# Chunked attention with a maxout layer in fp32: the last two token groups as one unit, their inner layers by seven block products for eight

## The chip, the cores and the metric

The kernel runs on one core of a Trainium2 chip. The metric is device microseconds of one execution. The engines are called as the profile calls them: PE is TensorE's matmul, PEld its weight load, DVE VectorE, ACT ScalarE, POOL GpSimd, SP SyncE, which issues the DMAs here.

## The reference

```python
# q, k, v: (8, 8, 576, 64) fp32; chunks of 64 positions
scores = scale * np.matmul(q_c, k_c.transpose(0, 1, 2, 4, 3))
attn = softmax(scores)                    # rows of 64, with 1e-9 added to the sum
x = (attn @ v_c) laid out as (4608, 512)  # tokens x d_model
h = np.maximum(np.maximum(x @ w1, x @ w2), x @ w3)   # 512 -> 768, three weights
out = h @ w_out                                      # 768 -> 512
```

Attention looks only inside a chunk, so 128 tokens of x (two chunks of all eight heads) can be made on their own. Then come three matrix products with an elementwise maximum, and one more product.

## The kernel before

**Precision.** A matmul operand is kept as two fp32r halves: a rounded high part and the rest, its low part. A product is then three matmuls, low times high, high times low and high times high, added up in one PSUM bank (`three`, L150 to L153). A high part is made on ACT by a cast, a low part by a subtraction on DVE or POOL.

**Tiles.** The 4,608 tokens are nine groups of 512. `wh` and `wl` hold the halves of the three weights in six column blocks of 128 (index j), `woh` and `wol` those of the last. For each group and each j, the three weights (index w) take 4 x 3 matmuls of 128x512 each into one bank (`hidden`). `maximum` evacuates the bank: ACT copies the first to the tile `m` (L431), DVE takes the greater of bank and `m` for the other two (L433). Then `high` (L439, ACT) and `low` (L442, DVE) make the halves `hh` and `hl`. After the six j, `project` multiplies these by `wout` in four blocks of 128 tokens, 6 x 3 matmuls each, and `output` copies and stores (L454, L455). A group has 288 such matmuls: 216 in the inner layers and 72 in the last.

**Attention.** A unit is 128 tokens, so 36 units. The first eight go through `plain_steps` in the first, hand-ordered stretch. The other 28 go through `attention`: loads of q and k (`r`), their halves (`qs`, `kk`), scores in two halves (`s`, L269) that share one PSUM buffer, evacuated by two ACT copies (L275) and two DVE additions (L280), the softmax steps, halves of the result (`ah`), a turn through DRAM (`there`, then `aa`), halves of v (`vs`, L287 and on POOL L291), two value products (`x`, L269) that share one buffer as well, and the halves of x (`xh`, `xl`, L394 and L399).

**Order.** The first stretch is the table `FIRST`. After it a list `parts` gives PE's matmuls, and every other step has a due time on a clock `now` that counts PE's work (0.6815 per three matmuls, 0.49 per attention product). A heap gives out the steps as they come due, and each engine runs its own in that order. Units of a group are due while the group ahead of it is on PE, 18.3 units of that clock apart. PSUM is used so: four banks in turn for the products, two for `s`, two for `x`.

## Time and profile before

| | us |
|---|---|
| median of 3 runs | 695.45 (695.07 to 703.29) |
| profiled execution, span from first to last instruction | 693.2 |
| the profiled execution's own time | not given; the nearest run, 695.07, is 1.9 above its span |
| PE busy | 687.0 (99%) |
| DVE, ACT, POOL busy | 449.2, 357.6, 150.7 |
| granted TensorE clock | 1.00 in the mean |

The share of an engine is its busy time by the span. The chain of waits names, for each stretch of the span, the engine on which the end depended. Rows of groups give a line, an engine, an operation and its tiles (written <- read), the number of instructions, the busy time, the mean ns of one, and the idle time ahead of them with what ended it. Rows of the timeline begin with the start and the duration in us. The first group lasts to about 120 us; from there to the end the eight other groups follow each other.

### The profile page before, as it was taken

How to read it: one execution, taken by the hardware profiler on the slowest of the kernel's cores; microseconds unless marked ns; L12 is line 12 of the kernel's file. 1: busy time of each engine (PE TensorE's matmuls, PEld its weight loads, DVE VectorE, ACT ScalarE, POOL GpSimd, SP SyncE). 2: the span in 40 equal slices, each digit the busy share in tenths (PEclk: the TensorE clock that was granted, in tenths of full speed). 3: DMA queues.
4: the chain of work that ended last, by engine and by line, in shares of the span. 5: the costliest groups of instructions: out<-in, count | busy, mean ns of one | idle time of the engine just before them, and what ended most of it. 6: DMA issues, size and time to landing. Idle time of an engine off the chain costs nothing.

```text
span 693.2 us, 9474 instructions
## 1 busy us (share of the span) xinstructions
PE 687.0 (99%) x3390; PEld 576.2 (83%) x3390; DVE 449.2 (65%) x805; ACT 357.6 (52%) x663; POOL 150.7 (22%) x107
## 2 busy tenths in 40 slices
PE   8999999999999999999999999999999999999997
PEld 5998888888888888888888888888888888888886
DVE  6999975767577766776577657775777567721220
ACT  4867645555655555555555555556555555431111
POOL 1422111212222222222222222221222222210000
PEclk9999999999999999999999999999999999999999
DMA  8955536455755576557655675557555765340001
GB/s 334 402 205 212 213 122 206 143 172 175 237 163 168 166 241 183 161 174 226 200 182 182 181 229 154 162 161 235 163 172 161 239 180 175 98 136 16 1 0 61
DMA packets 42351, 121.21 MB, mean 175 GB/s; under 512 B 3904, under 2 KB 3904, under 8 KB 42304
## 3 DMA queue, kind: packets, MB, share of 16 engines
q1 hardware_dynamic: 42304, 120.60, 54.3%
q8 instruction: 27, 0.44, 0.3%
q14 instruction: 20, 0.16, 0.1%
HBM read 96.47 MB, written 24.12 MB: 174 GB/s over the span
## 4 chain that ended last, share of the span: by engine, by line
PE 97%; DMA 2%; SPq 0%; ACT 0%; issue 0%
PE pm L151 29%; PE pm L153 28%; PE pm L152 28%; PE x L269 4%; PE s L269 4%; PE x L234 2%; PE s L191 1%; DMA buf<-in_vb 1%; DMA buf<-in_qk 1%; PE tp L223 0%; SPq L114 0%; ACT ao L454 0%; SPq L181 0%
## 5 line engine op out<-in xcount | busy, mean ns | idle before, releaser
L151 PE MATMUL pm<-xh,wl 128*128 128x512 f32 (+1 forms) x660 | 256.9, 389 | 0.0
L153 PE MATMUL pm<-xh,wh 128*128 128x512 f32 (+1 forms) x660 | 255.1, 386 | 0.0
L152 PE MATMUL pm<-xl,wh 128*128 128x512 f32 (+1 forms) x660 | 254.7, 386 | 0.0
L153 PEld LDWEIGHTS pm<-xh,wh 128*128 128x128 f32 x660 | 124.0, 188 | 26.5
L152 PEld LDWEIGHTS pm<-xl,wh 128*128 128x128 f32 x660 | 124.2, 188 | 22.1
L151 PEld LDWEIGHTS pm<-xh,wl 128*128 128x128 f32 x660 | 124.2, 188 | 22.0
L291 POOL TENSOR_TENSOR vs<-rv,vs 64x1024 fp32r<-64x1024 f32 x28 | 67.2, 2400 | 280.0 <-ACT vs L287 280.0
L280 DVE TENSOR_TENSOR e<-s,e 64x256 f32<-64x256 f32 x112 | 47.3, 422 | 102.5 <-ACT e L275 101.8
L433 DVE TENSOR_TENSOR m<-pm,m 128x512 f32<-128x512 f32 (+1 forms) x110 | 75.0, 682 | 38.1 <-PE pm L153 35.1
L151 PE MATMUL pm<-woh,hl 128*128 128x512 f32 x216 | 84.6, 392 | 0.0
L153 PE MATMUL pm<-woh,hh 128*128 128x512 f32 x216 | 84.3, 390 | 0.0
L152 PE MATMUL pm<-wol,hh 128*128 128x512 f32 x216 | 84.2, 390 | 0.0
L275 ACT COPY e<-s 64x256 f32<-64x256 f32 x112 | 41.2, 368 | 60.6 <-PE s L269 59.9
L275 ACT COPY xs<-x 64x256 f32<-64x256 f32 x112 | 41.1, 367 | 54.9 <-PE x L269 54.3
L439 ACT CAST hh<-m 128x512 fp32r<-128x512 f32 (+1 forms) x55 | 33.7, 613 | 69.2 <-DVE m L433 68.7
L280 DVE TENSOR_TENSOR xs<-x,xs 64x256 f32<-64x256 f32 x112 | 47.3, 422 | 25.2 <-ACT xs L275 23.5
L431 ACT COPY m<-pm 128x512 f32<-128x512 f32 (+1 forms) x55 | 31.8, 579 | 50.2 <-DVE hl L442 27.1
L153 PEld LDWEIGHTS pm<-woh,hh 128*128 128x128 f32 x216 | 40.5, 188 | 9.0
L152 PEld LDWEIGHTS pm<-wol,hh 128*128 128x128 f32 x216 | 40.6, 188 | 7.6
L151 PEld LDWEIGHTS pm<-woh,hl 128*128 128x128 f32 x216 | 40.6, 188 | 7.6
L168 POOL TENSOR_TENSOR e<-e,sm 128x512 f32<-128x512 f32 x30 | 31.3, 1043 | 68.3 <-DVE sm L165 68.3
L442 DVE TENSOR_TENSOR hl<-m,hh 128x512 fp32r<-128x512 f32 (+1 forms) x55 | 38.5, 699 | 5.7 <-ACT hh L439 4.8
(65 smaller groups left out, 756.6 us busy)
## 6 DMA issues: line engine op xcount, KB each, us to landing
r<-in_qk SPq DMA_DIRECT2D x56, 512.0 KB, 7.5
aa<-there SPq DMA_DIRECT2D x56, 512.0 KB, 5.9
rv<-in_v SPq DMA_DIRECT2D x28, 512.0 KB, 4.1
there<-ah SPq DMA_DIRECT2D x28, 512.0 KB, 2.6
out_x<-ao SPq DMA_DIRECT2D x36, 256.0 KB, 2.0
buf<-in_qk SPq DMA_DIRECT2D x8, 768.0 KB, 8.1
buf<-in_w SPq DMA_DIRECT2D x10, 512.0 KB, 4.1
buf<-in_vb SPq DMA_DIRECT2D x8, 512.0 KB, 5.7
```

What stands on the lines that cost most here:

```text
L151: nc.tensor.matmul(out=o, lhsT=al, rhs=bh, start=first, stop=False)
L152: nc.tensor.matmul(out=o, lhsT=ah, rhs=bl, start=False, stop=False)
L153: nc.tensor.matmul(out=o, lhsT=ah, rhs=bh, start=False, stop=last)
L168: eng.tensor_tensor(out=e, in0=e, in1=sm.unsqueeze(2).broadcast_to([P, 8, 64]), op=ALU.mult)
L269: nc.tensor.matmul(out=o[:, g].rearrange("p a h x -> p (a h x)"), lhsT=lhs(g), rhs=rhs(g), start=True, stop=True)
L275: nc.scalar.copy(out=out()[rows], in_=st[name][rows, :, 0, h, :])
L280: nc.vector.tensor_tensor(out=out()[rows], in0=st[name][rows, :, 1, h, :], in1=out()[rows], op=ALU.add)
L291: eng.tensor_tensor(out=st[name][64:], in0=src()[64:], in1=st[name][64:].bitcast(F32), op=ALU.subtract)
L431: nc.scalar.copy(out=banks[j][:, :n], in_=ps[j, w][:, :n])
L433: nc.vector.tensor_tensor(out=banks[j][:, :n], in0=ps[j, w][:, :n], in1=banks[j][:, :n], op=ALU.max)
L439: nc.scalar.copy(out=hh[j][:, lo:hi], in_=banks[j][:, :hi - lo])
L442: eng.tensor_tensor(out=hl[j][:, lo:hi], in0=banks[j][:, :hi - lo], in1=hh[j][:, lo:hi].bitcast(F32), op=ALU.subtract)
```

## The change

The last two groups, 1,024 tokens, become one unit (`pair`). Its inner layers are taken as 2x2 block matrices: two blocks of 256 input rows, two of 128 columns (blocks j = 2jp and 2jp+1), two of 512 tokens. Seven block products stand for the eight, in the variant with 15 block additions. One pair of column blocks jp and one weight w are a set; nine sets (jp 0 to 2, w 0 to 2), each 7 x 2 x 3 = 42 matmuls, where 48 stood.

- The tokens' side: b11, b21, b12, b22 are the four blocks of x in the tile `stage`. Four differences of them (`mix`, two on DVE, two on POOL) and the halves of seven operands (`high` on ACT, `low` on DVE, one on POOL) are made once (`operands`), each 128x1024.
- The weights' side (`combine`): per set, the two column blocks are made whole again from their halves (DVE; POOL for set 0), four sums of 128x256 on POOL, and their halves by ACT and DVE (the tile `c`).
- The results' side (`pair`'s `hidden`): per set, ACT copies products 1, 4, 5 and 7; DVE adds `u2` = product 6 + product 1; POOL makes `v`, `y` and `c22`; DVE makes c11, c12 and c21. For w > 0 DVE takes the greater with `m` four times, and for w = 2 the halves of the result follow (`H`, four casts and four subtractions).
- All 28 attention units are due ahead of the pair: the first four 18.0 apart as before, twelve 16.1 apart, twelve 14.0 apart. The last eight write their x into `stage`, unsplit.
- The pair's products go round eight banks (the four of `s` and `x` join). The last product of the pair starts with blocks 0 to 3 of three token blocks.
- Buffers move under other names; the scratch for DMA descriptors goes from 8192 to 1024. `FIRST` is the same.

```diff
+LATE = [0.0, 0.0, -1.2]
+EVERY = [18.3, 16.4, 14.6]
+OPERANDS = 5.0
+SECOND_MIXED = 1.6
+ORDER = (1, 2, 4, 5, 6, 3, 7)
+TIMES = [17.3 + 18.0 * n for n in range(4)] + [71.3 + 16.1 * (n + 1) for n in range(12)] + [282.0 + 14.0 * n for n in range(12)]
...
+    def combine(jp, w, homes, into, eng):
+
+        st = {}
+        a, b = 2 * jp, 2 * jp + 1
+        minus, plus = ALU.subtract, ALU.add
...
+        def whole(j, n):
+            def fn():
+                st[n] = homes[n]()
+                eng.tensor_tensor(out=st[n], in0=wh[j][:, w].bitcast(F32), in1=wl[j][:, w].bitcast(F32), op=plus)
+            return fn
...
+        def sum_of(n, x, y, op):
+            return lambda: nc.gpsimd.tensor_tensor(out=f32(n)(), in0=x(), in1=y(), op=op)
...
+        def high():
+            for k in range(2):
+                nc.scalar.copy(out=into()[:, 0, 2 * k:2 * k + 2], in_=st["c", k])
+
+        def low():
+            for k in range(2):
+                nc.vector.tensor_tensor(out=into()[:, 1, 2 * k:2 * k + 2], in0=st["c", k],
+                                        in1=into()[:, 0, 2 * k:2 * k + 2].bitcast(F32), op=minus)
+
+        return [whole(b, 1), whole(a, 0), sum_of(2, part(1, 0), part(1, 1), plus), sum_of(0, f32(2), part(0, 0), minus),
+                sum_of(1, part(0, 1), f32(0), minus), sum_of(3, part(0, 0), part(1, 0), minus), high, low]
...
+        def quarter(k, c):
+            return lambda: stage(c)[:, 2 * k:2 * k + 2]
+
+        b11, b21, b12, b22 = (quarter(k, c) for c in range(2) for k in range(2))
...
+        source = {1: b11, 2: b21, 3: b22, 4: room(0), 5: room(0), 6: room(1), 7: b12}
+
+        def mix(i, x, y, eng):
+            return lambda: eng.tensor_tensor(out=source[i](), in0=x(), in1=y(), op=minus)
...
+        def operands():
+            return [(0.0, mix(5, b12, b11, nc.vector)), (0.0, high(1)), (1.3, mix(6, b22, source[5], nc.vector)),
+                    (1.3, mix(7, b22, b12, nc.gpsimd)), (1.3, high(5)), (2.5, low(1)), (2.5, high(2)), (3.6, high(6)),
+                    (3.8, low(5)), (4.7, high(3)), (5.1, low(2)), (5.2, mix(4, b21, source[6], nc.gpsimd)),
+                    (5.8, high(7)), (6.3, low(6)), (7.7, low(3)), (7.7, low(7, nc.gpsimd)), (7.8, high(4)), (9.0, low(4))]
...
+        def weights(i, jp, w, k):
+            if i in (1, 2, 4):
+                j, ct = {1: (2 * jp, k), 2: (2 * jp, 2 + k), 4: (2 * jp + 1, 2 + k)}[i]
+                return wh[j][:, w, ct, :], wl[j][:, w, ct, :]
+            n = {6: 0, 3: 1, 5: 2, 7: 3}[i]
+            cols = slice(k * P, (k + 1) * P)
+            return ring[3 * jp + w][:, 0, n, cols], ring[3 * jp + w][:, 1, n, cols]
...
+            def copy(i, pool, tag):
+                def fn():
+                    st["s", i] = pool.tile([P, 512], F32, name=tag)
+                    nc.scalar.copy(out=st["s", i], in_=ps(i))
+                return fn
+
+            def u2():
+                st["u2"] = mp.tile([P, 512], F32, name="m")
+                nc.vector.tensor_tensor(out=st["u2"], in0=ps(6), in1=st["s", 1], op=plus)
+
+            def v():
+                nc.gpsimd.tensor_tensor(out=st["s", 5], in0=st["s", 5], in1=st["u2"], op=plus)
+
+            def y():
+                nc.gpsimd.tensor_tensor(out=st["u2"], in0=st["s", 7], in1=st["u2"], op=plus)
+
+            def c22():
+                if w:
+                    st["c", 7] = ao_p.tile([P, 512], F32, name="ao", tag="ao3")
+                nc.gpsimd.tensor_tensor(out=st["c", 7] if w else m(b, 1), in0=st["s", 5], in1=st["s", 7], op=plus)
...
+                    nc.vector.tensor_tensor(out=st["c", i] if w else m(j, c), in0=st["s", 4] if i == 4 else ps(i),
+                                            in1=st["u2"] if i == 4 else st["s", other], op=plus)
...
+            def greater(i, j, c):
+                return lambda: w and nc.vector.tensor_tensor(out=m(j, c), in0=st["c", i], in1=m(j, c), op=most)
...
+            turn = (1, 2, 5, 6, 3, 7, 4) if (jp, w) == sets[0] else (1, 4, 6, 5, 7, 2, 3) if (jp, w) == sets[-1] else ORDER
+            done = {i: 2 * STEP * (n + 1) + 0.3 for n, i in enumerate(turn)}
...
+            for i in turn:
+                st["ps", i] = bank()
+                for k in range(2):
+                    hi, lo = weights(i, jp, w, k)
+                    three(st["ps", i], hi, lo, X[i][0][:, k], X[i][1][:, k], k == 0, k == 1)
+                    yield []
...
+    for n, at_end in enumerate(done):
+        i, tt = 2 + n // 4, n % 4
+        first = at_end - 31.0
+        ops_of = stacked[2:3] + stacked[9:] if n == 0 else attention(
+            starts[i] + tt, lambda i=i: x_tiles(i), tt * P, EVERY[(n + 8) // 12],
+            None if i < last else lambda c=i - last: stage(c), LATE[(n + 8) // 12])
+        for at, pe, fn in ops_of:
+            plan(first + at, pe, fn)
+    both = pair(starts[last], stage)
...
+    for n, s in enumerate(both["sets"]):
+        part_after.append(both["hidden"](*s))
+        parts += [[("set", n)], part_after[-1]]
+    parts += [both["project"](0, 1, 2, before=4)] + [both["project"](tt) for tt in range(3, 8)]
...
+                for after, fn in list(zip((-1.6, -0.8, 0.3, 1.0, 1.7, 2.4, 3.3, 5.0), mixing[n]))[first:last]:
+                    plan(at + after, 0.0, fn)
...
+                    if what == "pair":
+                        for at, fn in both["operands"]():
+                            plan(now + OPERANDS + at, 0.0, fn)
+                    elif n < 0:
+                        plan_mixed(now + 1.6, 0, 0, 8)
+                    else:
+                        if n == 0:
+                            for p in reversed(pools.values()):
+                                p.__exit__(None, None, None)
+                            ps_u = ctx.enter_context(tc.tile_pool(name="ps_u", bufs=4, space=PSUM))
+                            both["places"][:] = [(ps_m, "pm")] * 3 + [(ps_t, "tp")] + [(ps_u, "pu")] * 4
+                        plan_mixed(now + SECOND_MIXED * (n == 0), n + 1, 0 if n == 0 else 2, 8)
+                        plan_mixed(now + 14 * STEP, n + 2, 0, 2)
```

What each engine's order becomes shows best on DVE and POOL. On DVE, group 8 of 9 in the kernel before, one attention unit long: the unit's steps with three maxima (L433) and one low part (L442) between them.

```order
L359 STREAM_TRANSPOSE et<-e 128x512
L280 TENSOR_TENSOR xs<-x,xs 64x4x64 x2
L368 TENSOR_TENSOR ah<-et,ah 128x2x256
L433 TENSOR_TENSOR m<-pm,m 128x512
L399 TENSOR_TENSOR xl<-xs,xh 128x4x128
L291 TENSOR_TENSOR qs<-r,qs 64x1024
L433 TENSOR_TENSOR m<-pm,m 128x512
L317 TENSOR_TENSOR kk<-r,kk 128x4x128 x2
L442 TENSOR_TENSOR hl<-m,hh 128x512
L280 TENSOR_TENSOR e<-s,e 64x4x64 x2
```

On DVE in the changed kernel, one whole set of the pair (jp = 1, w = 1) from its `u2` (L636) to the next set's: f are the weights made whole, c the sums' low parts (L516), ao or m from pm and xs or e the results c11, c12 (L655), m from xs and m c21, L661 the maxima, H a low part.

```order
L636 TENSOR_TENSOR m<-pm,xs 128x512
L493 TENSOR_TENSOR f<-wh_109,wl_115 128x512
L493 TENSOR_TENSOR f<-wh_108,wl_114 128x512
L655 TENSOR_TENSOR ao<-pm,e 128x512
L661 TENSOR_TENSOR m<-ao,m 128x512
L655 TENSOR_TENSOR m<-xs,m 128x512
L661 TENSOR_TENSOR m<-m 128x512
L655 TENSOR_TENSOR ao<-pm,xs 128x512
L661 TENSOR_TENSOR m<-ao,m 128x512 x2
L516 TENSOR_TENSOR c<-c 128x512 x2
L672 TENSOR_TENSOR H<-m,H 128x512
L636 TENSOR_TENSOR m<-pm,xs 128x512
```

Where DVE had a maximum or a low part now and then, it has 12 operations between two `u2`, ten of them with both inputs in SBUF.

POOL at the end of the kernel before: its last unit's three operations (scores less their maximum, normalisation, low part of v), and the end.

```order
L339 TENSOR_TENSOR e<-e,mx 128x512
L168 TENSOR_TENSOR e<-e,sm 128x512
L291 TENSOR_TENSOR vs<-rv,vs 64x1024
L598 UNCONDITIONAL_BRANCH
L598 ISA
```

POOL in the changed kernel, one set: `v` (L639), `y` (L642) and `c22` (L647), and between them the four sums (L508) for the set after.

```order
L639 TENSOR_TENSOR e<-e,m 128x512
L508 TENSOR_TENSOR c<-f 128x256
L642 TENSOR_TENSOR m<-et,m 128x512
L508 TENSOR_TENSOR c<-c,f 128x256
L508 TENSOR_TENSOR c<-f,c 128x256
L647 TENSOR_TENSOR ao<-e,et 128x512
L508 TENSOR_TENSOR c<-f 128x256
```

Seven operations per set, where POOL had none in the last group.

DVE where the units are 14.0 apart, in the changed kernel: the low part of q now stands directly behind the softmax's sum, ahead of the first value product's additions, and the second one's stand directly ahead of the next scores'.

```order
L172 RECIPROCAL sm<-sm 128x8
L298 TENSOR_TENSOR qs<-r,qs 64x1024
L287 TENSOR_TENSOR stage<-x,stage 64x4x64 x2
L366 STREAM_TRANSPOSE et<-e 128x512
L445 TENSOR_TENSOR m<-pm,m 128x512
L324 TENSOR_TENSOR kk<-r,kk 128x4x128
L375 TENSOR_TENSOR ah<-et,ah 128x2x256
L324 TENSOR_TENSOR kk<-r,kk 128x4x128
L454 TENSOR_TENSOR h<-m,h 128x512
L287 TENSOR_TENSOR stage<-x,stage 64x4x64 x2
L287 TENSOR_TENSOR e<-s,e 64x4x64 x2
```

Against the rows of before, the additions of two units now touch, with no other step between them.

193 lines of the change are left out of this document (170 added, 23 removed).

## The prediction

> **What bounds the kernel now.** I read the page first, then the end of the timeline, then the groups, then the places where DVE and POOL meet. The page's busy times and its chain of waits:
>
> ```profile
> span 693.2 us, 9474 instructions
> ...
> PE 687.0 (99%) x3390; PEld 576.2 (83%) x3390; DVE 449.2 (65%) x805; ACT 357.6 (52%) x663; POOL 150.7 (22%) x107
> ...
> PE 97%; DMA 2%; SPq 0%; ACT 0%; issue 0%
> ```
>
> PE is the bound: 97% of the chain is on it, and no other engine holds more than two thirds of the span. What a matmul costs is its pace, not its busy time. The timeline of the last products:
>
> ```profile
> 676.43 0.39 PE L151 MATMUL pm<-woh,hl 128*128 128x512 f32 x1
> ...
> 688.67 0.39 PE L151 MATMUL pm<-woh,hl 128*128 128x512 f32 x1
> ```
>
> Each L151 is the first of three, and they start 0.68 apart, so the two rows are 18 steps or 54 matmuls apart: 12.24 us, 0.2267 each. After the last one come a copy and a store, which the change keeps.
>
> The other engines' prices, from the groups by line:
>
> ```profile
> L433 DVE TENSOR_TENSOR m<-pm,m 128x512 f32<-128x512 f32 (+1 forms) x110 | 75.0, 682 | 38.1 <-PE pm L153 35.1
> L291 POOL TENSOR_TENSOR vs<-rv,vs 64x1024 fp32r<-64x1024 f32 x28 | 67.2, 2400 | 280.0 <-ACT vs L287 280.0
> ...
> L317 DVE TENSOR_TENSOR kk<-r,kk 128x512 fp32r<-128x512 f32 x56 | 36.3, 685 | 0.3
> ...
> L291 DVE TENSOR_TENSOR qs<-r,qs 64x1024 fp32r<-64x1024 f32 x28 | 34.2, 1223 | 3.0 <-ACT qs L287 2.3
> ...
> L439 ACT CAST hh<-m 128x512 fp32r<-128x512 f32 (+1 forms) x55 | 33.7, 613 | 69.2 <-DVE m L433 68.7
> ...
> L168 POOL TENSOR_TENSOR e<-e,sm 128x512 f32<-128x512 f32 x30 | 31.3, 1043 | 68.3 <-DVE sm L165 68.3
> ```
>
> These are means of operations that mostly ran alone. Where DVE and POOL both read SBUF at once, they don't. POOL's timeline, from four places:
>
> ```profile
> 9.81 1.27 POOL L146 TENSOR_TENSOR wl<-ao,wh 128x512 fp32r<-128x512 f32 x1 [8.50 <-ACT wh L143]
> ...
> 44.22 1.62 POOL L146 TENSOR_TENSOR wl<-ao,wh 128x512 fp32r<-128x512 f32 x1 [3.87 <-ACT wh L143]
> ...
> 70.35 1.31 POOL L140 TENSOR_TENSOR ao<-ao,buf 128x512 int32<-128x512 int32 x1 [5.08 <-DVE ao L135]
> ...
> 121.52 1.55 POOL L339 TENSOR_TENSOR e<-e,mx 128x512 f32<-128x512 f32 x1 [1.91 <-DVE mx L335]
> ```
>
> And DVE's at the last three of them:
>
> ```profile
> 44.02 0.68 DVE L146 TENSOR_TENSOR wl<-ao,wh 128x512 fp32r<-128x512 f32 x1
> ...
> 70.13 0.68 DVE L433 TENSOR_TENSOR m<-pm,m 128x512 f32<-128x512 f32 x1
> 70.73 0.68 DVE L159 TENSOR_REDUCE sm<-e 128x8 f32<-128x512 f32 x1
> 71.33 0.89 DVE L146 TENSOR_TENSOR wl<-ao,wh 128x512 fp32r<-128x512 f32 x1
> ...
> 121.47 0.69 DVE L442 TENSOR_TENSOR hl<-m,hh 128x512 fp32r<-128x512 f32 x1
> ```
>
> Four readings. A POOL operation of 128x512 with two full inputs takes 1.27 alone. Begun while a two-input SBUF operation of DVE runs, it ends 1.14 after that one: L146 at 44.22 ends at 45.84, DVE's ended at 44.70; and L339 at 121.52 ends 0.91 after DVE's, against the 1.04 of its like (L168), the same 0.13 less. Begun while POOL runs, DVE's ends 0.56 after POOL's (72.22 against 71.66). A DVE operation with an input from PSUM or with one input does not wait (70.73 beside POOL's 70.35). Back to back, DVE's start 0.60 apart. So the two share one way to SBUF, in turn.
>
> The Trainium skill ("SBUF — State Buffer", Who interferes with whom) has the rule: a VectorE instruction with two SBUF inputs and a GpSimd instruction that reads SBUF exclude each other, and the second blocks until the first finishes. The trace agrees, but for the fixed part of about 0.13 that overlaps; by the rule without overlap the floor worked out below would be 109.7 us, not 91.7.
>
> **What goes.** Two groups hold 576 of the 128x512 matmuls; the pair has 9 x 42 + 144 = 522. The 54 fewer are 54 x 0.2267 = **12.24 us** off PE. Attention keeps its matmuls. Nothing else leaves PE, so this is also the most that can be gained.
>
> **Attention sooner.** Its seven groups of room become six. The stretch with units 18.4 apart:
>
> ```profile
> 270.00:340.00 70.00, 70.00 (x336) 58.78 (x335) 47.15 (x85) 38.66 (x73) 16.65 (x11) 1.00 0.59 179
> ```
>
> DVE is busy 47.15 of 70. A group of 73.5 us has 12 maxima and 6 low parts, 12.3 us, or 11.7 in this window; the other 35.5 are 3.81 units, 9.3 each. At 14.0 apart a unit brings 9.3 and 2.3 of the group's: 11.6 of 14.0, 83%. POOL has two of 1.04 and one of 2.40, 4.5 of 14.0. The DMAs at 0.59 of their time go to 0.59 x 18.4 / 14.0 = 0.78, on SP's one queue. All three still fit. Whether PE waits depends on the scores, whose halves share a buffer. Chain and DVE timeline of one unit:
>
> ```profile
> 353.71 0.47 PE s L269 x4
> ...
> 356.93 0.47 PE s L269 x4
> ```
> ```profile
> 355.06 0.86 DVE L280 TENSOR_TENSOR e<-s,e 64x256 f32<-64x256 f32 x2 [1.40 <-ACT e L275]
> ```
>
> The additions end at 355.92, 1.01 ahead of the second half. The changed order may eat that margin; between 0 and 1 us for each of 12 units I take 0, for PE's own waiting would give DVE the time back, and keep 3 us for the range.
>
> **Operands of the pair.** Eight DVE operations of 128x1024 (1.22) and three of POOL (2.40, or 2.27 behind DVE's) exclude each other: 8 x 1.22 + 3 x 2.27 = 16.6 us, due from 5 us into the 72 matmuls (16.3 us) of the group ahead. They end some 4.5 us into the first set. The product that needs the last of them is that set's seventh, 6 x 1.36 = 8.2 in. So 0; if attention ran 3 us late it would still be about 0.
>
> **The sets.** PE needs 42 x 0.2267 = 9.52 per set, 28.56 for w = 0, 1, 2. DVE has 3 sums from PSUM, and with both inputs in SBUF 5, 9 and 13: two blocks made whole, two low parts of c, c21, then four maxima, then four low parts of H. POOL has three of 1.27 and four of 128x256; between the 2.40 for 1024 elements and the 1.27 for 512 a line gives 0.71 for 256 (0.58 behind DVE's).
>
> One interval between two `u2`, for w = 1, by DVE's order and turn by turn. From the first `u2`'s end: whole b to 0.60; v, which waited for it, to 1.74; whole a to 2.29; first sum to 2.87, c12 beside it; y to 4.14; maximum of c12 to 4.69; second sum to 5.27; c21 to 5.82; third sum to 6.40; its maximum to 6.95; c22 to 8.09, the next c11 beside it; fourth sum to 8.80; two maxima to 9.95; two low parts of c to 11.15; one of H to 11.75; u2 to **12.35**. Without the maxima and H (w = 0) it is **10.3**. With all four low parts, one of which waits for ACT's cast (0.61), it is **13.7**. Together 36.4, where PE needs 28.56. Who is bound by whom has changed here: each set's c must be there when PE comes to its first product with it, 4.08 into the set (2.72 in the last).
>
> From PE's start of the pair: u2 of set 0 at 6.8, set 1 at 19.6 (it has set 1's own c to do too, 12.8), then 31.9, 45.6, 55.9, 68.3, 82.0 and 92.3. The c of the following set is there 0.6 earlier, or 1.2 where an H stands between. For sets 1 to 3 that is 10.6, 19.0 and 30.7, and PE asks at 13.6, 23.1 and 32.6: no wait, the lead is used up. Set 4: 45.0 against 42.2, 2.8 late. Then, each counted from the delayed PE: 55.3 against 54.5 (0.8), 67.1 against 64.8 (2.3), 81.4 against 76.6 (4.8), 91.7 against 89.5 (2.2). That is 12.9. The eight banks don't bind ahead of this: PE gets no more than a set ahead.
>
> **The end.** PE's last set ends at 98.5. Blocks 0 to 3 of three token blocks cover 36 matmuls, to 106.7. The last `u2` ends at 99.1; v, y and c22 follow, c21, two maxima, the rest, and the first low part of H at 107.35: another 0.65.
>
> **Sum.** 12.9 + 0.65 - 12.24 = +1.3. On this execution 693.2 becomes 694.5; the median lies 2.25 above the span, so **697**, no change.
>
> **Bounds.** Below: DVE's 77 two-input operations at 0.55, POOL's 27 at 1.14 and 32 at 0.58 are 42.4 + 30.8 + 18.6 = 91.7 us that nothing can run side by side. From 4.3 on that ends at 96.0, where PE would be at block 4 at 85.7 + 8.2 = 93.9. So at least 2.1 are lost, at most 10.1 gained: 685. Above: POOL starts 0.14 after its releaser, as these rows of DVE and POOL show, and ACT's casts may come as late:
>
> ```profile
> 363.19 0.20 DVE L165 RECIPROCAL sm<-sm 128x8 f32<-128x8 f32 x1
> ```
> ```profile
> 363.53 1.04 POOL L168 TENSOR_TENSOR e<-e,sm 128x512 f32<-128x512 f32 x1 [2.54 <-DVE sm L165]
> ```
>
> Five such hand-overs in nine sets are 6.3, and with 3 from attention 706.
>
> **Rivals.**
> 1. *The shared way is hidden.* DVE's PSUM operations always fall beside POOL's, and PE's lead covers the rest: between 2.1 and 7 us lost, 685 to 690. For it: only 0.8 to 2.8 us are missing in sets 4 to 6, and another order of turns may save as much. Against: DVE must go through its list in order, and between the fourth sum and the next v POOL has nothing it may do. Chance 0.28.
> 2. *Attention becomes the bound, slower.* Low part of q (1.22) and POOL's normalisation (1.04) both fall behind the sum, both need the shared way, and one waits for about 1.0. What follows is 0.86 + 0.86 of additions ahead of the scores', whose margin was 1.01. If DVE is over 1.0 late at the unit's start, PE waits at the second half. At 0.7 for each of 24 units closer than 18 apart that is 17 more: 714; at half, 705. For it: 83% of DVE on paper, with the collision 90%. Against: the maxima can lag four banks. Chance 0.12.
> 3. *Fewer products in name alone.* PE's order has 54 matmuls fewer; no chance.
>
> The forecast's own case, 691 to 704, has 0.58; 0.02 is for what I don't see. 2% is about what a measurement of this kernel can tell from no change, that is 681.5 and 709.4. Faster than that needs more than the 12.24 that leave PE: 0.03. Slower is the half of rival 2 and a little: 0.07. Same: 0.90. The range, 685 to 706, takes in rival 1 and leaves out most of rival 2.
>
> **What would show it.** PE's idle time should be near 13 us, all in the last 120 us, ended by the low parts of c (DVE); means there above 0.69 for DVE's maxima and low parts and above 1.27 for POOL's 128x512; `u2` to `u2` near 36 for three sets. With rival 1, PE stays near 99% busy and the pair takes some 120 us. With rival 2, PE's waits stand at `s` and `x` between 150 and 540 us. I am wrong if DVE and POOL run side by side without stretching, or if PE waits on something I have at zero: operands, banks, or SP's queue.

## The result, and the profile after

The changed kernel takes 743.27 us in the median of 4 runs (740.37 to 747.51), the kernel before beside it 699.37 (695.07 to 704.23). The ratio is 1.063, with a 95% interval of 1.055 to 1.072: slower, by some 44 us, and outside the range of the prediction. The profiled execution has a span of 740.3 at a mean granted clock of 0.977, against 693.2 at 1.000.

The page of the changed kernel, busy times and chain of waits:

```profile
span 740.3 us, 9601 instructions
...
PE 697.0 (94%) x3336; PEld 574.1 (78%) x3336; DVE 538.5 (73%) x875; ACT 382.7 (52%) x704; POOL 245.4 (33%) x175
...
PE 49%; DVE 19%; DMA 12%; ACT 6%; POOL 6%; issue 6%; SPq 1%; POOLq 0%; DVEq 0%; ACTq 0%
```

PE has its 54 matmuls fewer (3336 for 3390) and still holds only half of the chain, where it held 97%. A DMA holds 12%, though the DMA engines are no busier than before (the page gives the queue's packets 52.0% of their time, 54.3% before).

**Where the time went.** One cut through the span answers it: the start of the pair's first matmul and the last matmul's row, in PE's timeline.

```profile
603.44 0.39 PE L158 MATMUL pm<-X,wl 128*128 128x512 f32 x1
...
736.18 0.39 PE L160 MATMUL pm<-woh,H 128*128 128x512 f32 x1
```

In the kernel before, the last three matmuls end at 688.67 + 3 x 0.2267 = 689.35. Take off the two groups that are now the pair (576 x 0.2267 = 130.6), and PE would have done all attention and seven groups at 558.7. Now it gets there at 603.44: **44.7 us are lost ahead of the pair.** The pair itself takes 133.1 to its last matmul's end; 576 plain matmuls are 130.6. So the part of the kernel that the change is named after costs 2.5, and the rest is in the stage that the prediction set at nothing.

PE's waits, over the whole span (us in total, times, the longest), and busy times of two stretches (length, then PE, PEld, DVE, ACT and POOL with their instructions, granted clock, share of the DMAs, GB/s): the units planned 14.0 apart, and the sets of the pair.

```profile
PE x L276 <- DMA aa<-there: 19.8, 10, 4.2
PE s L276 <- DVE e L287: 6.3, 7, 3.4
PE pm L158 <- DVE c L516: 6.2, 4, 2.1
```
```profile
352.00:604.00 252.00, 227.76 (x1039) 186.81 (x1039) 177.11 (x290) 132.49 (x246) 82.11 (x49) 0.95 0.62 174
604.00:703.00 99.00, 90.84 (x380) 72.86 (x379) 87.36 (x95) 33.26 (x61) 67.69 (x57) 0.97 0.01 5
```

The largest wait is of the value products `x` for the transposed weights `aa`. From 352 to the pair PE has 14 waits. They come to 24.2 by the profile, and to 26.5 when each is counted from where the matmul ahead of it ends at its pace of 0.2267. The matmuls at half pace (below) add 8.4, the seven waits of the units before (from 168) 4.4 by the same count, and the rest of the 44.7 is in smaller gaps. No engine is full there: DVE is busy for 177 of 252 us, the DMAs for 0.62 of the time.

**One such wait, followed back.** The chain of waits in the changed kernel, from a unit's last softmax sum to its value product (start, us, what):

```profile
385.80 0.04 DVE sm L172
...
386.04 0.69 DVE m L445
...
386.76 0.69 DVE qs L298
...
388.31 0.71 DVE et L366
389.02 0.57 DVE h L454
389.59 0.60 DVE kk L324
390.19 0.61 DVE ah L375
...
390.83 2.70 DMA there<-ah
...
394.24 9.92 DMA aa<-there
...
404.30 1.19 PE x L276 x4
```

Between the reciprocal (which ends at 386.00) and the weights' low part `ah`, DVE does a maximum, the low part of the following unit's q, a low part of `h` and one of `kk`: 4.8 us to `ah`'s end. The low part of q is the one of which rival 2 spoke: it met POOL's normalisation (386.15 to 387.20) and took 1.52, where it takes 1.22 alone. Then come the store, two loads behind a load of `r`, and PE, which waited from 400.13 on.

This unit was late before that, and by more. Its reciprocal ended 16.2 after its first scores, where the eleven others of the last twelve units have 9.3 to 10.8, because its second scores came 6.8 behind the first and not 3.2. DVE's, POOL's and PE's timelines show what held them up:

```profile
370.60 2.90 DVE L324 TENSOR_TENSOR kk<-r,kk 128x512 fp32r<-128x512 f32 x1
```
```profile
370.38 2.57 POOL L298 TENSOR_TENSOR vs<-rv,vs 64x1024 fp32r<-64x1024 f32 x1 [7.26 <-ACT vs L294]
```
```profile
376.56 1.19 PE L276 MATMUL s<-kk,qs 128*128 128x256 f32 x4 [3.42 <-DVE e L287]
```

A low part of k, 0.68 alone, was begun while POOL made its low part of v, and ended 0.55 after that one; a maximum and the scores' additions stood behind it. So the first wait over 1 us of this stage is at the scores' shared buffer, and what brings it about is the way to SBUF that DVE and POOL share. Before it, from 352 on, PE had no wait at all. Of the 11.1 us by which this unit's weights land later than before (34.4 after its first scores for 23.3), 6.4 are the reciprocal's, 1.2 are `ah`'s, and the transfers have the rest.

The kernel before has the same chain. Its DVE, SP and PE timelines, for one unit, whose `aa` landed at 376.89:

```profile
366.24 0.69 DVE L368 TENSOR_TENSOR ah<-et,ah 128x512 fp32r<-128x512 f32 x1
```
```profile
366.96 0.33 SPq L373 DMA_DIRECT2D there<-ah  x1
369.63 1.24 SPq L380 DMA_DIRECT2D aa<-there  x2
```
```profile
377.69 0.64 PE L269 MATMUL x<-aa,vs 128*128 128x256 f32 x4
```

`ah` ends 3.54 after the reciprocal (363.39), and the weights land **0.80 ahead** of PE's asking. That margin, 0.4 to 1.1 in the 15 units 18.37 apart from 316 to 574, stands in no list of waits, because nothing waited. The change used it up twice: the table asks for the value products 1.2 earlier, and `ah` comes later. Over the last twelve units `ah` ends 6.2 after the reciprocal, where it was 3.55; the reciprocal itself comes 0.6 later after the scores (nearly all of it from the unit above), and the transfers take 0.5 and 0.6 longer. The weights land 27.6 after the unit's first scores instead of 23.3, and the units come 17.26 apart, where 14.0 was planned.

### The profile page after: what moved, and what is told of

It is laid out like the page before. It is cut to its first block, busy times and chain, and to the rows that moved or that the text cites. A ratio compares the mean times of both kernels' runs of the same rounds, so it can differ in the third digit from the quotient of the medians.

```text
span 740.3 us, 9601 instructions
## 1 busy us (share of the span) xinstructions
PE 697.0 (94%) x3336; PEld 574.1 (78%) x3336; DVE 538.5 (73%) x875; ACT 382.7 (52%) x704; POOL 245.4 (33%) x175
## 4 chain that ended last, share of the span: by engine, by line
PE 49%; DVE 19%; DMA 12%; ACT 6%; POOL 6%; issue 6%; SPq 1%; POOLq 0%; DVEq 0%; ACTq 0%
PE pm L158 14%; PE pm L159 14%; PE pm L160 14%; DMA aa<-there 8%; PE x L276 3%; DMA there<-ah 3%; PE s L276 3%; DVE m L661 2%; DVE m L445 2%; POOL c L508 2%; DVE e L287 2%; ACT e L282 1%; DVE kk L324 1%; POOL e L346 1%; DVE sm L166 1%
## 5 line engine op out<-in xcount | busy, mean ns | idle before, releaser
L158 PE MATMUL pm<-xh,wl 128*128 128x512 f32 (+1 forms) x516 | 204.3, 396 | 0.0
L159 PE MATMUL pm<-xl,wh 128*128 128x512 f32 (+1 forms) x516 | 202.4, 392 | 0.0
L160 PE MATMUL pm<-xh,wh 128*128 128x512 f32 (+1 forms) x516 | 202.0, 391 | 0.0
L158 PE MATMUL pm<-woh,h 128*128 128x512 f32 x168 | 65.8, 392 | 0.0
L159 PE MATMUL pm<-wol,h 128*128 128x512 f32 x168 | 65.6, 390 | 0.0
L160 PE MATMUL pm<-woh,h 128*128 128x512 f32 x168 | 65.6, 390 | 0.0
L276 PE MATMUL x<-aa,vs 128*128 128x256 f32 x224 | 38.6, 296 | 20.1 <-DMA aa<-there 19.8
L276 PEld LDWEIGHTS x<-aa,vs 128*128 128x128 f32 x224 | 34.1, 195 | 29.8 <-issue 19.7
L346 POOL TENSOR_TENSOR e<-e,mx 128x512 f32<-128x512 f32 x28 | 31.1, 1110 | 45.6 <-DVE mx L342 45.6
L276 PEld LDWEIGHTS s<-kk,qs 128*128 128x128 f32 x224 | 33.7, 191 | 15.8 <-ACT e L282 4.9
L287 DVE TENSOR_TENSOR xs<-x,xs 64x256 f32<-64x256 f32 x80 | 33.6, 421 | 15.1 <-ACT xs L282 13.9
L276 PE MATMUL s<-kk,qs 128*128 128x256 f32 x224 | 37.2, 289 | 7.6 <-DVE e L287 6.3
```

Of the source, the lines that this page charges most:

```text
L158: nc.tensor.matmul(out=o, lhsT=al, rhs=bh, start=first, stop=False)
L159: nc.tensor.matmul(out=o, lhsT=ah, rhs=bl, start=False, stop=False)
L160: nc.tensor.matmul(out=o, lhsT=ah, rhs=bh, start=False, stop=last)
L276: nc.tensor.matmul(out=o[:, g].rearrange("p a h x -> p (a h x)"), lhsT=lhs(g), rhs=rhs(g), start=True, stop=True)
L287: nc.vector.tensor_tensor(out=out()[rows], in0=st[name][rows, :, 1, h, :], in1=out()[rows], op=ALU.add)
L346: nc.gpsimd.tensor_tensor(out=e_all(), in0=e_all(), in1=st["mx"].unsqueeze(2).broadcast_to([P, 8, 64]), op=ALU.subtract)
```

## The experiments

All are compared by the span of their profiled execution. Each is a single run, but for `spread_banks` with four; the runs of the kernel before beside them have spans of 693.0 to 703.1, the changed kernel's own four 738.6 to 745.7. "First set" is the start of the pair's first matmul, "pair" the time from there to the end of the last one.

| run | span | first set | pair | clock |
|---|---|---|---|---|
| changed kernel | 740.3 | 603.4 | 133.1 | 0.977 |
| late0 | 735.7 | 597.4 | 134.5 | 0.981 |
| lead2 | 721.5 | 583.2 | 134.5 | 0.988 |
| prep3 | 720.0 | 583.0 | 133.2 | 0.995 |
| spaced | 695.3 | 558.8 | 132.4 | 0.999 |
| prep3_lead2 | 732.4 | 594.2 | 134.5 | 0.980 |
| both | 723.5 | 585.2 | 134.5 | 0.990 |
| spread | 751.0 | 613.4 | 133.8 | 0.981 |
| early | 747.9 | 610.2 | 133.9 | 0.979 |
| ahead | 716.4 | 579.5 | 133.2 | 0.992 |
| ahead_prep3 | 709.4 | 572.4 | 133.2 | 0.998 |
| nosums | 715.4 | 593.0 | 118.6 | 0.986 |
| maxbank | 717.4 | 584.2 | 129.4 | 0.998 |
| banks | 720.5 | 586.9 | 129.8 | 0.993 |
| spread_banks | 748.2 | 613.7 | 130.8 | 0.984 |
| early_banks | 741.6 | 608.6 | 129.2 | 0.988 |

In the expectations D is the theory that PE's wait for the transposed weights makes the loss; R and "rival" stand for what each text says against it.

**Asking later, by little and by more.** `late0` takes back the 1.2, `lead2` asks 3.2 later than the changed kernel, both counted from the unit's scores.

```diff
-LATE = [0.0, 0.0, -1.2]
+LATE = [0.0, 0.0, 0.0]     # late0
+LATE = [0.0, 0.0, 2.0]     # lead2, with the last twelve due from 280 on, not 282
```

> The changed kernel with the value products of the last twelve attention units due 1.2 later, as they stood before the change. Theory D (the turn through DRAM lands after PE asks for it): PE waits up to 1.2 us less in each of the twelve units, some 14 us in all, span near 726 to 730 instead of 740.3. Rival R (an engine or the DMAs cannot do a unit in less than the 17.3 us measured): the units stay 17 us apart, span 740 within 4.

> The changed kernel with the last twelve units begun 2.0 earlier and their value products due 3.2 later than in it, counted from the unit's scores. Theory D: PE asks 3.2 us later for what lands 4 to 5 us late, so most of the 36 us lost in this stretch come back and the granted clock stays at 1.00 there: span 705 to 715. Rival R: no change of the 17.3 us a unit, span 740 within 4.

`late0` gains 6.0 ahead of the pair, `lead2` 20.3. The direction is D's, the sizes are not: both fell short, and `late0`'s span lies between the two forecasts, next to R's. Its 6.0 alone is within the scatter of single runs, but the list of waits changes with it: PE's wait for `aa` falls from 19.8 to 9.7, while its value products now wait 6.3 for additions. What PE does not wait for the weights it partly waits for elsewhere. `lead2` also has no collision of `kk` with POOL's low part of v, so not all of its 20.3 is the later asking. PE's waits in `lead2`:

```profile
PE x L276 <- DMA aa<-there: 7.2, 5, 3.5
...
PE s L276 <- DVE kk L324: 2.5, 3, 1.6
```

**Making the weights sooner.** `prep3` brings loads and halves of the following unit's q and k 3.0 earlier in the last twelve units, out from between the reciprocal and `ah`.

```diff
-            @due(at)
+            @due(at - prep)          # r; the same for qs and kk; prep 3.0 for the last twelve
```

> The changed kernel with loads and halves of q and k 3.0 earlier in the last twelve units, so that DVE makes them ahead of the softmax's sum and not between it and the halves of the result. Theory D with DVE's order as the cause of the lateness: these halves are ready near 14 us after the scores instead of 16.1 in the mean, PE's wait falls by 1.5 to 2.5 us a unit, span 712 to 724. If lateness comes from the DMAs alone, or from a rate (R): 740 within 5.

The span is as expected, the way to it only in part. `ah` now ends 4.2 after the reciprocal, the weights land 25.2 after the scores, and the units come 15.6 apart. So the order on DVE is worth about 20 of the 44.7; PE still waits 11.0 us in 11 places for `aa`, which it asks for as early as before. That is 8.8 less, 0.7 a unit and not 1.5 to 2.5. The rest of the gain is elsewhere: `kk` no longer falls beside POOL's low part of v, the wait of 3.42 at the scores is gone, and of the matmuls at half pace 8 are left.

**Room instead of 14.0.** `spaced` leaves out the last four units; of the 24 that stay, the first four are due as before and the other 20 stand 17.6 apart. It also takes back the 1.2, as `late0` does.

```diff
-LATE = [0.0, 0.0, -1.2]
-EVERY = [18.3, 16.4, 14.6]
+LATE = [0.0, 0.0, 0.0]
+EVERY = [18.3, 18.0, 18.0]
-TIMES = [...] + [71.3 + 16.1 * (n + 1) for n in range(12)] + [282.0 + 14.0 * n for n in range(12)]
+TIMES = [...] + [71.3 + 17.6 * (n + 1) for n in range(20)]
```

> The changed kernel without the last four attention units (the last 512 tokens take the x of the 512 ahead of them), so that the other twenty stand 17.6 apart; the pair is untouched. If the packing of attention is the whole of what was not forecast, the first set starts near 551 (the 603.4 measured, less 44.7 of waits and slower clock, less 7.7 of PE's work for four units) and the pair takes the 133 us it took: span 686 to 692. If buffers, banks or the queue's smaller scratch cost time by themselves, the stretch ahead of the pair still loses 10 us or more.

The four units left out are 4 x 4 x 0.49 = 7.8 us of PE's work on the table's clock, so without loss the first set would start at 550.9. It starts at 558.8: 7.9 lost, between the two forecasts. `late0`, whose value products are due at the same place in a unit, loses 38.7, the changed kernel 44.7. The wait for `aa` is 1.1 us in 3 places. So most of the loss comes with the close spacing.

**The margin in the kernel before.** `before_x24` is the kernel before, with the value products and the halves of x behind them due 2.4 earlier.

```diff
-            products((24.0, 27.7)[c], (25.0, 29.3)[c], "ps_x", "x", ...
+            products((21.6, 25.3)[c], (22.6, 26.9)[c], "ps_x", "x", ...
```

> The kernel before, with the value products and what follows them due 2.4 earlier and nothing else changed. Theory D says that its units had only 0.4 to 1.1 us between the landing of the turn through DRAM (23.3 us after the scores) and PE's asking (24.1): asked at 21.7, PE waits about half of the lack in each unit (the wait of one gives time to the next), 0.8 in 27 units, span 710 to 718. If there was more room than the landings show: 693 within 3.

Its span is 762.5, where 693.2 stood, and PE's waits are these:

```profile
PE x L269 <- DMA aa<-there: 40.2, 19, 3.2
PE x L269 <- POOL vs L291: 15.0, 9, 1.8
```

So the old kernel had next to no room at this place: the edit alone, with units due 18.4 apart as before, costs 69 us, about three times what was expected. The units come 20.3 to 20.6 apart for the most part, 20.8 in the mean. The first value product now stands directly ahead of the next unit's second scores; a wait there delays the next softmax, and so that unit's weights (the scores' halves start 5.7 apart for 3.22). POOL's part of the halves of v, which the edit overtook too, adds its own wait.

**Both edits together.** `prep3_lead2` joins the two that gave 20 each.

> Both moves together: q and k prepared 3.0 earlier, value products asked for 3.2 later in the last twelve units. Theory D: the turn through DRAM then lands 24 to 26 us after the scores and PE asks at 26.1, so nearly no wait is left at the value products: first set near 566 (within 4), span 699 (within 5). If the two moves only shift one and the same wait elsewhere, the first set stays near 583 as with either alone.

It came to 594.2, worse than either. One unit's load of k stood in the order a moment ahead of the last read of the k before, so a unit's low parts were made from the next unit's keys, and PE waited 3.7 us behind it, at the second scores; `both` softens the step for one unit (the edit reaches eleven units at 3.0, not seven as its text says), but the next unit's load has the same fault by 0.1 on the table's clock. Both runs, and the three that stand on them (`nosums`, `maxbank`, `banks`), are to be read with that.

> The changed kernel with the last units' value products and attention weights asked for 3.2 later in the table (+2.0 instead of -1.2) and the loads and halves of the following unit's queries and keys 3.0 earlier in the last seven units (1.5 in the unit before those, none before it). D (the 44.7 us ahead of the pair come from the transposed weights not having landed when TensorE reaches their value products): both edits act on it, one by asking later, the other by making the halves sooner, so landing comes before the asking in nearly all of the last units; lead alone gave 583.2 for the pair's first set and preparation alone 583.0, together 566 to 572, the span 700 to 706. Rival (the rest of the loss is a limit of VectorE's and GpSimd's own work in a unit, which no order of due times removes): the first set stays at 580 or later, the span at 715 or over.

Here the two edits give 585.2, no more than one of them. The softmax's reciprocal, which in nine of the last ten units of `prep3` came 10.2 to 11.1 after the scores, comes 11.2 to 14.7 after them in nine of the last ten here: asked so late, the second value product stands between the first and the second scores of a later unit, and each wait there delays that unit's softmax. The rival's number holds. Whether its reason (the engines cannot do it) holds too was still open.

**Even spacing.** A group's operand tile is shared with the group two before it, so the first unit of a group can't write its rows until that group is through; that is what holds the last twelve units back to 282 on the table's clock. `spread` lets two units wait with that write alone, and spaces 24 units 15.2 apart. The loads and halves of q and k are due 1.3 later, behind `ah`, as before; value products 2.0 later. `early` is `spread` with the loads and halves 3.0 earlier than the changed kernel has them (1.5 in the fifth unit).

```diff
+TIMES = [17.3 + 17.0 * n for n in range(4)] + [68.3 + 15.2 * (n + 1) for n in range(24)]
+LATE = [0.0, 2.0, 2.0]
+EVERY = [17.3, 15.5, 15.5]
+HOLD = {5: 215.5, 6: 281.5}    # copies of the finished rows not ahead of this
# prep as in prep3, from the fifth unit on: -1.3 in spread, 1.5 and then 3.0 in early
```

> The changed kernel with another table for attention: the first four units 17.0 apart, the other 24 evenly 15.2 apart (in the changed kernel 16.1, and 14.0 for the last twelve); value products 2.0 later in the table from the fifth unit on; the halves of the following queries and keys 1.3 later, so that the low part of q again stands behind the weights' low part on VectorE as in the kernel before; the write of the finished rows of two units into their group's operand tile, which a group still at work holds, waits in the table until that tile is free. The same instructions, and the pair untouched. D (the 44.7 us are an order of work inside the unit that does not fit 14.0, plus TensorE's waits for the transposed weights that it causes): periods near 15.8, waits ahead of the pair under 10 us, the first set at 560 to 568, the span 693 to 701. Rival (VectorE, GpSimd and the stores and loads together cannot do 28 units and the layers in that room, whatever the order): the first set stays beyond 578, the span beyond 711.

> As the run named spread, but the halves of the following queries and keys 4.3 earlier in the table (3.0 earlier than in the changed kernel from the sixth unit on), so that none of them stands between the weights and the additions on VectorE, and they are there long before TensorE asks. Order theory (spread lost 15.2 us of PE's waits to the keys' halves and 16.8 to the additions of the value products, which stood behind q's low part): both kinds of wait nearly go, waits for the transposed weights stay small because the value products are asked 2.0 later; first set at 565 to 575, span 698 to 708. Volume theory (28 units do not fit in that room): first set beyond 583, span beyond 716.

Both are slower than the changed kernel, and both leave next to no wait for the weights. PE's waits at the value products and scores, in `spread`, then in `early`:

```profile
PE x L277 <- DVE xs L288: 16.8, 14, 2.4
PE s L277 <- DVE kk L325: 15.2, 17, 1.7
...
PE x L277 <- DMA aa<-there: 0.6, 2, 0.4
```
```profile
PE x L277 <- DVE xs L288: 24.4, 14, 2.6
PE x L277 <- DVE stage L288: 6.0, 5, 2.7
...
PE x L277 <- DMA aa<-there: 1.2, 2, 0.7
```

In `early` the second value product waits for the additions of the first, whose buffer it needs. DVE's and PE's timelines of `early` at one such place:

```profile
478.52 0.70 DVE L367 STREAM_TRANSPOSE et<-e 128x512 f32<-128x512 f32 x1
479.14 0.64 DVE L325 TENSOR_TENSOR kk<-r,kk 128x512 fp32r<-128x512 f32 x1
479.90 0.69 DVE L376 TENSOR_TENSOR ah<-et,ah 128x512 fp32r<-128x512 f32 x1
480.54 0.86 DVE L288 TENSOR_TENSOR stage<-x,stage 64x256 f32<-64x256 f32 x2
```
```profile
481.55 0.71 PE L277 MATMUL x<-aa,vs 128*128 128x256 f32 x4 [2.71 <-DVE stage L288]
```

The additions stand behind the chain of the other unit's weights on DVE's queue, and that chain is itself late. So three chains compete for the order on one queue: weights to `x`, additions to the second `x`, halves to the next scores.

These two tables also bring a collision that neither text foresaw: the low part of x falls due together with POOL's low part of v, and DVE waits for POOL. The line in the changed kernel and in `spread` (shortest, median and longest in ns, first and last start):

```profile
L411 DVE TENSOR_TENSOR xl<-xs,xh x20: 681/692/695, 130.1 to 461.7; 128x512 fp32r<-128x512 f32 x20
```
```profile
L412 DVE TENSOR_TENSOR xl<-xs,xh x20: 678/2522/2796, 129.3 to 473.5; 128x512 fp32r<-128x512 f32 x20
```

In `early` the median is 2511. In each of the two runs 13 of the 20 are stretched, some 23 us of DVE's time in all, with scores' additions behind them (in `spread` from 307.31 on: 2.52 of low part, a maximum, and the additions at 310.47). How much of the slowness hangs on this was not tried, so the two runs do not tell whether units 15.2 apart can be held. D's number is missed in both; the rival's holds, but no engine is full: from 352 to 560 DVE is busy for 150 of 208 us in `spread`.

**The wait alone.** `ahead` changes nothing in DVE's order. In the last twelve units the loads of `aa` take the weights of the unit before and are queued ahead of the unit's own store.

```diff
-        @due(15.5)
+        @due(12.6 if late else 15.5)
+            there = loaded["there"]      # the store of the unit before
```

> The changed kernel, where the last twelve units load the transposed weights of the unit before theirs (a store long landed), queued ahead of their own store: as many loads of the same size, which no longer wait for this unit's weights; the values are those of the wrong unit in the last twelve. The suspected wait taken away, all else as it is. D (the 44.7 us are that wait and the slow clock behind it): TensorE's waits for the transposed weights nearly go, periods 14.3 to 15, the first set at 560 to 570, the span 697 to 708. Rival (VectorE's queue in order is next: additions of the value products or halves of the keys, late for the same reason, take over): the first set at 580 or later, with TensorE's waits at the additions or the keys' halves.

> As the run named ahead (the last twelve units use the weights of the unit before theirs), and the loads and halves of the following queries and keys 3.0 earlier in those units, as in prep3. In ahead 20.8 us stay: 4.8 in the units at 16.1, 11.4 of waits in the last twelve, 9.6 of them for the scores' additions on VectorE (put down as late because q's low part, the keys' low parts and POOL's normalisation stand ahead of them). If the halves are what makes those additions late, they come on time: the first set at 566 to 572, the span 703 to 709. If not (another order of the same work on VectorE makes something else late), it stays at 577 to 583.

`ahead` starts the pair at 579.5: **23.9 of the 44.7** are the wait for the weights and what hangs on it (SP, too, no longer waits for the store ahead of the loads). That is more than half; D had expected it to be all; the rival's 580 is missed by half a microsecond. What PE waits for now is the place that rival 2 of the prediction named, the second scores' shared buffer. The longest of these waits, 3.4, stands behind the same collision of `kk` with POOL's low part of v as in the changed kernel:

```profile
PE s L276 <- DVE e L287: 9.6, 12, 3.4
...
PE x L276 <- DMA aa<-there: 1.2, 3, 0.7
```

`ahead_prep3` takes the halves out from ahead of those additions too. PE's waits, and the busy times from 352 to 560:

```profile
PE x L277 <- DMA aa<-there: 3.4, 6, 1.7
PE s L277 <- DVE e L288: 1.6, 4, 0.7
```
```profile
352.00:560.00 208.00, 203.87 (x987) 169.15 (x986) 165.32 (x286) 124.49 (x237) 77.39 (x46) 1.00 0.73 208
```

The scores' waits fall from 9.6 to 1.6, the first set comes at 572.4 (expected 566 to 572), seven units in the middle of the stage 13.6 to 14.4 apart, the clock at 1.00. DVE is busy for 165.3 of 208 us, 79%, the DMAs for 0.73. So the engines can do units some 14 apart while PE is fed; what was lost is order and latency, not volume. The 13.7 left to 558.7 are 0.3, 5.5 and 5.1 of waits (before 168, to 352, to the pair; counted at the pace, as above), and smaller gaps.

**The pair.** `nosums` makes the weights' operands for the first set alone and uses them for all nine; `maxbank` lets 18 of 24 maxima read a PSUM bank, without regard to which. Both stand on `prep3_lead2`, whose pair took 134.5.

```diff
-            if n < len(both["sets"]):                                     # nosums
+            if n == 0:
-                return lambda: w and nc.vector.tensor_tensor(out=m(j, c), in0=st["c", i], in1=m(j, c), op=most)   # maxbank
+                return lambda: w and nc.vector.tensor_tensor(out=m(j, c), in0=st["c", i] if i == 7 else ps(2 if i == 2 else 3), in1=m(j, c), op=most)
```

> As the run with both moves, but the weights' block sums are made once, for set 0, and used for all nine sets: 16 DVE operations that make weights whole, 16 low parts, 32 POOL sums and their casts are left out. Theory P (DVE and POOL, taking turns at SBUF, bind the pair): with them gone each set's list fits into PE's 9.52 us, u2 to u2 is 9.5, and the pair takes 119 to 121 us instead of 133. Rival: the pair is bound by banks or by the latency behind its last product, and stays above 129.

> As the run with both moves, but 18 of the 24 maxima read one operand from a PSUM bank and not from SBUF, so that they do not exclude POOL (the values are other ones; the number of DVE operations is the same). Theory P, turn by turn: u2 to u2 falls from 12.4 to 11.5 behind a w = 1 set and from 13.9 to about 12.3 behind a w = 2 set, the pair from 133 to about 126. Rival: DVE's amount of work alone binds, and nothing changes (within 1 us).

Without the sums the pair takes 118.6, which is 522 x 0.2267 = 118.3: PE alone, no wait. With fewer operations of two SBUF inputs the intervals between two `u2` fall from 12.4 and 13.9 to 11.5 and 12.7 (expected 11.5 and 12.3), and the pair takes 129.4 (expected about 126). DVE has as many operations as before, so it is not their number alone that binds. `banks` and the two like it get there with no maximum left out or misplaced: c11, c12 and c21 are written back into their bank (the maxima are with `m`, not with zero as the text of `banks` has it).

```diff
+                    if w:
+                        st["c", i] = ps(i)
-                    nc.vector.tensor_tensor(out=st["c", i] if w else m(j, c), in0=st["s", 4] if i == 4 else ps(i),
+                    nc.vector.tensor_tensor(out=st["c", i] if w else m(j, c), in0=ps(i),
```

> As the run named both, and in the pair three of the four combined blocks are written back in place into a PSUM bank instead of into SBUF, so that the maxima with zero that follow read PSUM: VectorE's operations with two SBUF inputs fall from 27 to 18 in three sets. If the turns of VectorE and GpSimd at SBUF set the pair's 133 us: 126 to 128 from the first set to TensorE's end, the time before the pair unchanged. Rival (TensorE's own products set the pair): 131 to 134, unchanged.

> As the run named spread, and in the pair three of the four combined blocks written in place into a PSUM bank, so that the maxima behind them read PSUM. D: the first set at 560 to 568, 126 to 130 from there to TensorE's end (the run named banks has 129.4, the one named both 134.2), the span 688 to 698, the kernel before within 2%. Rival as for spread: beyond 706.

> As the run named early, with three of the four combined blocks in a PSUM bank: 4 to 5 us less from the first set to TensorE's end (both to banks 134.2 to 129.4, spread to spread_banks 133.4 to 130.4). Order theory: span 694 to 704; volume theory beyond 712.

The pair falls by 4.7, 3.0 and 4.7 us (134.5 to 129.8, 133.8 to 130.8, 133.9 to 129.2), less than expected by some 2 us in `banks`. The first set's sums and the hand-overs stay, which may be why. The maxima that now read PSUM no longer stretch; DVE's group in `banks`, from 585 to 700:

```profile
L659 DVE TENSOR_TENSOR m<-pm,m 128x512 f32<-128x512 f32 x18 | 12.3, 688 | 0.4
```

This improvement to the pair held in all three pairings. It does not make up for the attention: `spread_banks` is slower than the kernel before by a ratio of 1.076 (1.068 to 1.084), and no kernel that was tried with all of its work beats the kernel before.

One caution on all of these: the attention of `prep3_lead2`, `nosums` and `maxbank` is the same, and their first sets start at 594.2, 593.0 and 584.2. The other pairs with equal attention agree within 1.7 us. Differences under some 10 us between single runs are therefore held to mean something only where the list of waits changes with them, as from `ahead` to `ahead_prep3`.

## Why the prediction was wrong, point by point

- **What goes: right.** 54 matmuls fewer, and `nosums` shows the 522 that remain at 0.2267.
- **Attention sooner: the step that failed.** "Whether PE waits depends on the scores, whose halves share a buffer ... I take 0 ... and keep 3 us for the range." It measured 44.7. In these runs PE waits for attention at five places: the halves of k (`kk`) and the buffer (`e`) of the scores, the weights (`aa`), the halves of v (`vs`) and the buffer (`xs`, `stage`) of the value products. The step looked at the scores' buffer alone, and set at nothing what came to 6.3 us of waits there, 3.42 of them in one. The costliest is the value product's weights, which come by the longest chain of the unit, with 0.4 to 1.1 us in hand. `before_x24` shows that asking 2.4 sooner is enough to lose 69 us with no change of the due spacing (40.2 of PE's waits are for `aa`, 15.0 for `vs`), and `ahead` that the wait for these weights, with what hangs on it, is 23.9 of the 44.7 here. The order rows shown in front of the prediction had q's low part directly behind the reciprocal; the step on rival 2 priced that collision for the scores and did not follow it to `ah`. POOL's low part of v, 2.40, was counted as POOL's work, and not as time that an operation of DVE may have to wait.
- **The shares of DVE and the DMAs: right, and beside the point.** 83% and 0.78 were worked out for units at 14.0; `ahead_prep3`, which comes closest to that spacing, has 79% and 0.73. That they fit was taken to mean that PE would not wait. It does not follow.
- **"PE's own waiting would give DVE the time back": half wrong.** A wait of PE at `x` just ahead of the second scores delays the next softmax, and the next weights with it. In `both` and `before_x24` that is seen: a wait breeds the next one.
- **Rival 2: the right side, at a third of the price.** It asked for waits at `s` and `x` between 150 and 540 us, and they are there; it put them at 8 to 17 us, through the scores' additions. In the changed kernel these are 6.3, in `ahead` 9.6, and the first long wait is one of them. Most of the loss is at `x`, for which it had no price. The collision it named (low part of q with the normalisation) is in the trace at 386.15, and took 0.30 there; the one behind the long wait is of a low part of k with POOL's low part of v.
- **The operands: right.** Their exclusive turns stretch three operations of DVE to 3.4 us and three of POOL to 3.3 to 3.4, and no product of the first set waits for them.
- **The sets: right, but for a wait of 1.9 for a bank.** From the pair's start the ends of the nine `u2` are 6.3, 19.8, 32.2, 46.1, 56.5, 68.9, 82.7, 93.0 and 100.0, where the prediction has 6.8, 19.6, 31.9, 45.6, 55.9, 68.3, 82.0, 92.3 and 99.1. The view of that line in the changed kernel gives first and last start; DVE's groups from 604 to 712 show the stretching that it forecast, and who escapes it:

```profile
L636 DVE TENSOR_TENSOR m<-pm,xs x9: 678/684/692, 609.1 to 702.8; 128x512 f32<-128x512 f32 x9
```
```profile
L661 DVE TENSOR_TENSOR m<-ao,m 128x512 f32<-128x512 f32 x18 | 20.4, 1146 | 1.4 <-POOL ao L647 1.2
...
L655 DVE TENSOR_TENSOR m<-xs,m 128x512 f32<-128x512 f32 x9 | 12.6, 1405 | 4.8 <-POOL m L642 4.8
...
L636 DVE TENSOR_TENSOR m<-pm,xs 128x512 f32<-128x512 f32 x9 | 6.2, 684 | 0.3 <-PE pm L160 0.3
```

  PE's gaps over 0.5 in the pair are 10.4 and its slow matmuls 3.0, together 13.4 where 12.9 + 0.65 was forecast; the pair took 133.1 for 131.9. Of these waits 6.2 by the profile end with a low part of c, as forecast. Another 1.9, at 645.85 and 681.88, are for a bank, which the prediction had at nothing ("The eight banks don't bind"): the third product of a set goes, by the round of eight, into the bank of the second product of the set before, and DVE's c11 (L655) read that one until 645.79 and 681.83. Rival 1 is out: the shared way is not hidden, and `nosums` shows that with the weights' sums gone PE waits for nothing in the pair.

Without the attention's 44.7 the sum would have been right within 2 us. The range failed because a term that rested on one buffer was allowed 3 us of it.

**What stays open.** No order of the same work was found that keeps PE fed with all 28 units in that room; `ahead_prep3` shows that the engines have the time, but it uses the weights of the unit before. Asking for the value products a whole unit later, with their own weights, would be the version of it that leaves nothing out; it was not tried. With `ahead_prep3`'s first set and the pair of `early_banks` it would end near 705 (an estimate from these two runs), still behind the kernel before.

## What to carry to other kernels

When a change puts the same steps closer together, list every place where the bounding engine takes something over from another, and read in the trace how long before its use each thing is there: a kernel with no waits may have half a microsecond in hand, and the list of waits doesn't show it. Shares of busy time say whether work fits; whether it comes in time is told by the longest chain of one unit and by what stands ahead of each of its steps on an in-order queue. A wait that stands ahead of the start of the next unit's chain is paid again in that unit.

## What the runs showed of the hardware

A wait of PE costs more than its length. PE's timeline in the changed kernel, ahead of and behind the wait of 4.17 us shown above:

```profile
399.73 0.39 PE L160 MATMUL pm<-xh,wh 128*128 128x512 f32 x1
404.30 1.19 PE L276 MATMUL x<-aa,vs 128*128 128x256 f32 x4 [4.17 <-DMA aa<-there]
405.29 0.63 PE L158 MATMUL pm<-xh,wl 128*128 128x512 f32 x1
405.71 0.63 PE L159 MATMUL pm<-xl,wh 128*128 128x512 f32 x1
...
409.85 0.39 PE L160 MATMUL pm<-xh,wh 128*128 128x512 f32 x1
```

The matmuls behind it start 0.43 apart, not 0.23, for over 4 us, and then come back to 0.23. There are 42 such matmuls in the attention stage, 42 x 0.2 = 8.4 us, a fifth of the loss; the clock of 0.95 from 352 to 604 is this. The Trainium skill ("TensorE: Matmul & The Clock Gate", Part 1) says that TensorE falls to half its clock after an idle window of about 3.4 us and needs a busy one of that length to come back; this row agrees in size. The trace adds that some shorter waits have it too: behind the wait of 2.71 us in `early`, shown above, matmuls from 483.68 to 485.81 start 0.43 apart. In the changed kernel the same is seen behind waits of 2.65 and 2.60 and, in the pair, of 1.94 and 2.12, but not behind those of 1.89 and 2.18 ahead of the pair.

DVE and POOL take turns at SBUF so regularly that a list of operations in order, with 0.55 or 0.60 for DVE's and 1.14 or 1.27 for POOL's, gave the time of nine sets to within 1%. The transfers through DRAM are less even: from the issue to the landing of `aa` the median went from 5.9 to 6.3 us, but the longest from 7.4 to 9.9, with a load of `r` issued 1.29 ahead of it.
